# Strassen's seven products for the second feed-forward product of the last two batches

## The chip, the cores and the metric

The kernel runs on one NeuronCore of a Trainium2 chip. Its engines are TensorE (PE; the loads of its stationary operand are listed apart as PEld), VectorE (DVE), ScalarE (ACT), GpSimd (POOL) and SyncE (SP), which issues most of the DMAs. Each engine works through its own instructions in a fixed order, and semaphores hold an instruction until what it needs is there. The metric is device time in microseconds (us) of one execution.

## The reference

Eight batches of 576 tokens and 512 features go through three stages:

```python
# attention: 8 heads of 64, window of 128 keys, ALiBi slopes
scores = where(mask, q @ k.T / 8 + slope * -|i - j|, -1e9)
x = concat_heads(softmax(scores) @ v)            # 8 x 576 x 512
# Fourier mixing and a norm
u = x + real(fft(fft(x, axis=1), axis=2))
un = (u - mean(u)) / sqrt(var(u) + 1e-6)
# feed-forward
out = u + relu(un @ w_ch1) @ w_ch2               # 512 -> 2048 -> 512
```

## The kernel before

The batches b = 0 to 7 follow one another on every engine, and the stages of neighbouring batches overlap: while PE does the feed-forward products of batch b, DVE and ACT do the softmax of batch b + 1. Everything is float32 outside; where a factor goes through PE it is split into a high and a low float16 half, and a product is three passes: high by high, high by low, low by high.

The feed-forward (`ffn`, L951 to L985) takes the tokens of a batch in parts: two parts of 256 rows, and after each odd batch a third part of 128 rows, in which the remainders of two batches stand together. For a part, the first product (L965) walks over the 16 blocks of 128 hidden features, two blocks to one bank of PSUM (a "group" below): 2 blocks x 4 chunks x 3 passes = 24 matmuls of 256 columns. ACT writes the ReLU's high half (`upper_half`, L945) and DVE the low half (`lower_half`, L948) into a slot of the tile `hbuf`. When all 16 blocks are there, the second product (L979) is run for each of the two tiles of 128 rows: 16 blocks x 3 passes = 48 matmuls, `hbuf` stationary (128 x 128) and w2 streaming through with 512 columns, into one bank. One DVE instruction scales the bank and adds the residual, and a DMA writes the tile out.

The order of all instructions is written out by hand: functions put their steps into a list `waiting`, sorted by a due time (constants such as `FORWARD`, L53, one due time for the feed-forward of each batch), and the table `ORDER` says which entry of that list is taken next (`sequence()`, and the loop at its end that ties each engine to this order). DVE, ACT and POOL are recorded through one helper, so all their instructions carry the line L247 (L254 in the changed kernel); they are told apart by tiles. Other lines that matter: L295 (preparation of w1 at the start), L496 (scores), L572 to L580 (products with v), L702 and L766 (Fourier mixing, rows and columns), and the loads L269 (w), L404 (q), L405 (k) and L428 (v), which SP issues.

Names in the rows: `fp` is a bank of PSUM of the feed-forward, `sp` of the scores, `pv` of the products with v, `pd` of the Fourier mixing; `wall` holds the split weights (and other things at the start), `uT` the transposed normed rows, `X` the rows of a batch, `P` and `pt` the scores after the softmax and transposed, `fg`, `pm`, `abcd`, `fh`, `fl`, `zh`, `zl` steps of the Fourier mixing.

Of the kernel before, what the change touches and what calls it, by code (L numbers as in the profile page):

```python
# [108 lines left out]
09y1+-uRO>{9nY+CrQMaV+O_-cmlmMQM~wGc4Mks>V(#RM*DrQ+U^S>o9Oh!BwtNcJ$>QqJuy77H7?YVXxQO`+Ivn6Awuyy>LA{l
ksDqalbtEGbIR+Ra;%{EJ9@WkYE#Jb3pLKxdJc>S3+n2X&9Y&oyOhtkVtxFTRJ&s>8<4%|l*5J^!E3V~q2RpJNEO0D=coYlJL2w@  # L110
*DuPpl&bGSj=xl9VJm&RWJYV7{nYo|g-4H37T8bjtd!Y2^8|)RXpk4c^PXP7Gxv6~)wh{Hz-Nz&ef?a@ovdY}vrU&=ISILT9%W+}
^wDFs37ebT2p~p8{9aPBRP>IV_B-pH6DM=>|4Maxd_J)eh^`lmxGPoAYsIq#Pm_6+yUUf6Ae)Bg4|!ivS((K9mEeqgzm!Ek%V#We
j?XppUVdV6ljE4PIuE|T>PFA`?Knp|%@y*Q7q1kBoQn+f1Y#a_%@XgF<(VjQTIUK{P=+ZoM}0lP(kqfmx}%WSdy$8Ape0ZF@Ip4k
bx|Wvcd2?yk@b;h&(g^T&lb5AbU!m?LsRB_N*Q#{n99ap&lL<A-ZAaaBy&&5drvXY=q4r#s?@tJpJqI`7kRA^RW~Oo5(Wxt%`$r(
S6*mzZYSmwJW*#UQsytJRu+VT;-ltx+!7COq`G@ZJtHf(FR8ZT8KtwJ^D~Vjp6Qw2?6ELO@bjR1Y4M$G%e{?Fr(Qfe{;cz9y|k(O
$IscLX!5DQg-&8!Zal0~=QKU%>ABC7qTI^l<HFN}Gv*w7#<x@M5o_XE&qy{9#ur*TT)C~q??bjXL$2GDk|wu(zS1jas#M=e`P5g%
34WrjROQ?4ORGK9Je79VdM9ytn{%{Dj$I0BReqbSDK|N4a#~i*vUfSd?cP#<V}S~u?wHbc`1#SE_9uDiJNgZUs=MK)+6id(H|NiS
Vw;w}{?!|(Ro57ErlfuD>HnSVZmF{(sLov|+cVk&&lk3e-&d@7)XJ|c=-(YxGfO$x6uqP@Uyz?OW1h38t~j#SPuF;y9+W3=EgW;~
=Fz5mg{88}Ub%=mkv%B>nW*Bq5r(`HJW|Bgk>?h9k4xfcrYcWEJ(a5TPP>J2VPocM$Fy3fT!op6e#xtuDznpwuiG3i`<d}UvHv8G
NPho@az0XX?`KNLN<ueL^tV*(H)kBu>x6eYVKvhU)InA9rQ(%^p3Jg;=chPt`^K6#ahBJ!)A=*Mi~Joaqfl_IB6|~o8LL*OqsFpm  # L120
gQAE&SAEKC@jdS_*0)nWqt1RxI`P#ACqW)$L97SKU8$OEkt4&Ap0)WTN6G_Cvd#`Sr@6{(eXeIeg6c6vJ}+0^_{n9i8CAKeA3lot
;zx6Zk8<zvqxRSD%iNOGH;PlstPhHtw@bylX@)fN3R$GindQt|$}CJYlV>Nd@oUJ@M4RWX<e$|yIVsnV9u0fNF=n_sRZ5cmxK@i=
Wxt{##`Z^We6{jrrd+(KM-?}5f2uu|H+8_`BYNM`<!`zEn1(<0DQ^1z-r4`}q51y-%a6_SKf)L;y8
"""


def begin_of(p):
    b, j = divmod(p, 4)
    return BEGIN[b] + 6 * PACE[b] * j


def transform_of(b):
    return BEGIN[b] + PACE[b] * DFT
# [1053 lines left out]
```

## Time and profile before

| | us |
|---|---|
| three runs | 1024.91, 1021.87, 1024.29 (median 1024.29) |
| the profiled execution, its own time | 1021.92 |
| its span in the profile | 1020.1 |
| PE busy | 994.9 (98% of the span) |
| DVE busy | 717.0 (70%) |
| ACT busy | 565.6 (55%) |
| POOL busy | 28.5 (3%) |

The span is 1.8 us shorter than the execution's own time. The busy times are averages over the whole span; the stages differ: DVE is nearly full in some stretches and nearly idle from 870 us on, where only the feed-forward of batch 7 is left. Matmuls overlap each other in the records, so the mean duration of one matmul in the table of groups (379 ns for 512 columns) is longer than the distance from one to the next; that distance is read from the chain of waits, where a run of matmuls stands with its total time and count.

### The profile page before, as it was taken

Reading aid. Unit: us, or ns where it says so; the run is one execution under the profiler, and the core shown is the slowest. Engines: PE = TensorE matmul, PEld = TensorE weight load, DVE = VectorE, ACT = ScalarE, POOL = GpSimd, SP = SyncE. Lnnn points to the kernel's source line nnn. Section 1 sums busy time; section 2 is a strip of 40 time slices with the busy share of each in tenths; the row PEclk is TensorE's granted clock in tenths of the full one; section 3 lists DMA queues with packets and bytes.
Section 4 is the critical chain, followed back from the end, with each engine's and each line's share of the span. In section 5 each row is a group of like instructions: output and inputs, shape, how many; then the busy total and the mean of one; then the engine's idle time right before and its main releaser. Section 6 shows DMA issues by size and latency. Waiting matters only on the chain.

```text
span 1020.1 us, 23193 instructions
## 1 busy us (share of the span) xinstructions
PE 994.9 (98%) x9192; PEld 712.0 (70%) x9192; DVE 717.0 (70%) x2166; ACT 565.6 (55%) x1229; POOL 28.5 (3%) x68
## 2 busy tenths in 40 slices
PE   6998999999999999999999999999999999999998
PEld 5887767767666775858585785858586785857756
DVE  4799999896878978677988458688797793501111
...
PEclk9999999999999999999999999999999999999999
...
GB/s 357 273 255 175 40 141 83 73 156 97 135 55 139 96 133 63 93 112 57 120 95 111 53 72 97 56 91 142 126 49 101 77 45 11 63 22 1 21 11 22
DMA packets 189389, 99.86 MB, mean 98 GB/s; under 512 B 163552, under 2 KB 171744, under 8 KB 189280
## 3 DMA queue, kind: packets, MB, share of 16 engines
...
## 4 chain that ended last, share of the span: by engine, by line
PE 78%; DVE 11%; DMA 5%; ACT 3%; issue 2%; POOL 0%; SPq 0%; ACTq 0%; DVEq 0%; POOLq 0%
PE fp L965 31%; PE fp L979 31%; PE sp L496 3%; PE pd L702 3%; DVE wall L247 2%; DVE P L247 2%; PE sp L494 2%; PE pv L578 1%; DMA pt<-P 1%; PE pv L572 1%; DMA uT<-un 1%; PE pv L580 1%; PE pv L579 1%; PE pd L766 1%; ACT wall L247 1%
## 5 line engine op out<-in xcount | busy, mean ns | idle before, releaser
L979 PE MATMUL fp<-wall,hbuf 128*128 128x512 f16 x1728 | 391.8, 379 | 0.3 <-DVE hbuf L247 0.3
L965 PEld LDWEIGHTS <-wall 128*128 128x128 f16 x3840 | 339.0, 98 | 46.9 <-issue 8.1
L965 PE MATMUL fp<-uT,wall 128*128 128x256 f16 x3072 | 350.5, 273 | 3.1 <-DMA uT<-un 1.0
L979 PEld LDWEIGHTS <-hbuf 128*128 128x128 f16 x1728 | 162.4, 98 | 180.7 <-issue 2.3
L247 ACT ACTIVATE hbuf<-fp 128x512 f16<-128x512 f32 (+1 forms) x145 | 85.6, 590 | 209.5 <-PE fp L965 206.2
L247 ACT ACTIVATE P<-P,nb 128x256 f32<-128x256 f32 (+1 forms) x320 | 143.3, 478 | 74.6 <-DVE nb L247 70.8
L247 DVE SCALAR_TENSOR_TENSOR hbuf<-fp,hbuf 128x512 f16<-128x512 f32 x144 | 98.8, 686 | 95.4 <-ACT hbuf L247 94.9
L247 DVE CUSTOM_DVE_ANT_0 P<-sp,rg,nsl 128x256 f32<-128x256 f32 (+1 forms) x260 | 110.6, 450 | 13.2 <-PE sp L496 10.1
L247 DVE SCALAR_TENSOR_TENSOR P<-P 128x384 f16<-128x384 f32 (+1 forms) x104 | 63.9, 618 | 19.4 <-ACT P L247 19.3
L247 ACT ACTIVATE P<-P 128x384 f16<-128x384 f32 (+1 forms) x104 | 58.5, 570 | 22.1 <-DMA pt<-P 17.8
L247 DVE SCALAR_TENSOR_TENSOR X<-fp,misc,X 128x512 f32<-128x512 f32 x32 | 23.8, 744 | 60.7 <-PE fp L979 60.7
L578 PE MATMUL pv<-vhs,pt 128*128 128x65 f16 x468 | 54.2, 195 | 1.2 <-DMA pt<-wall 0.9
L579 PE MATMUL pv<-vl,pt 128*128 128x64 f16 x468 | 54.1, 192 | 0.0
L580 PE MATMUL pv<-vhs,pt 128*128 128x65 f16 x468 | 54.0, 193 | 0.0
L578 PEld LDWEIGHTS <-pt 128*128 128x128 f16 x468 | 43.6, 97 | 11.8 <-issue 3.7
L247 ACT ACTIVATE un<-X,nmr,rstd 128x512 f16<-128x512 f32 (+1 forms) x56 | 42.3, 804 | 13.9 <-DVE nmr L247 12.4
L579 PEld LDWEIGHTS <-pt 128*128 128x128 f16 x468 | 43.4, 99 | 5.2
L496 PE MATMUL sp<-kk,qq 64*128 64x256 f16 (+1 forms) x780 | 45.4, 260 | 0.0
L965 PE MATMUL fp<-wall,wall 128*128 128x128 f16 x768 | 44.1, 219 | 0.0
L580 PEld LDWEIGHTS <-pt 128*128 128x128 f16 x468 | 43.6, 97 | 0.0
L496 PEld LDWEIGHTS <-qq 64*128 64x128 f16 x780 | 32.7, 94 | 15.4 <-issue 10.5
L702 PE MATMUL pd<-tab_sb,fh 96*128 96x289 f16 (+1 forms) x168 | 36.8, 287 | 0.0
(178 smaller groups left out, 1206.6 us busy)
## 6 DMA issues: line engine op xcount, KB each, us to landing
...
out_dram<-X SPq DMA_DIRECT2D x32, 256.0 KB, 2.1
...
pt<-P SPq DMA_TRANSPOSE x104, 3.1
```

Of the source, the lines that this page charges most:

```text
L247: add(now[0], lambda: f(*a, **kw))
L494: T.matmul(sp[e][:m, col:col + n], lhs, keys(kk, ti), start=True, stop=True)
L496: T.matmul(sp[e][:m, col:col + n], qq[h, c0:c0 + m], keys(kk[h], ti), start=(x == 0), stop=(x == len(prods) - 1))
L572: T.matmul(pv[:, ti], pt[:, col:col + 128], vrs[p][:, e, vc], start=first, stop=last)
L578: T.matmul(pv[:, ti], ph, vh[:, e, vc], start=first, stop=False)
L579: T.matmul(pv[:, ti, 0:D], ph, vl[:, e, vc], start=False, stop=False)
L580: T.matmul(pv[:, ti], pl, vh[:, e, vc], start=False, stop=last)
L702: T.matmul(zp[:, :NS], st["in", c][l][:m, g], tab1_sb[:m, (0 if g < 2 else 2) + t, c], start=(c == 2 and p == 0), stop=(c == 1 and p == 2))
L766: T.matmul(o, st[z, g][:, j0:j0 + m], tab2_sb[:, t, gc[g]:gc[g] + gw[g]], start=(p == 0), stop=(p == 2))
L965: T.matmul(fp[:, i * n:(i + 1) * n], w1_ap(e, c, f0 + i), uT[:, j, c, 0:n], start=(c == 0 and p == 0), stop=(c == 3 and p == 2))
L979: T.matmul(op, hh[f][:, a, i * 128:(i + 1) * 128], w2_ap(e, f), start=(f == 0 and p == 0), stop=(f == 15 and p == 2))
```

## The change

For the two parts of 256 rows of batches 6 and 7, the second product is computed by Strassen's method in its seven-product form. Each part's rows are two tiles of 128, the columns of w2 two halves of 256, and the hidden blocks are taken in pairs; of this 2 x 2 by 2 x 2 block product seven products of blocks (each three passes of 128 x 128 by 256 columns: 21 matmuls a group) stand where eight were (12 matmuls of 512 columns a group). They accumulate in four banks of the scores (`sp`). What is multiplied are sums and differences of blocks:

- of the activations, once for each group of each part (`row_sums`): ACT writes the ReLU to a tile r, DVE makes four sums of 128 x 128 in a tile s, ACT copies the high half of s, DVE writes the low half. There is one r and one s, tiles named `vr`.
- of w2, once for each of the eight groups, for both batches (`second_sums`, `second_differences`, `second_halves`): six DVE instructions and two ACT copies. The results stand in tiles of the attention (`rg`, `kk`, `qq`, `P`, `pt`), the work in a tile of `X`. The constant `SUMS` puts them at a due time.
- of the seven results, once for each part (`add_up`): one ACT and seven DVE instructions where two DVE instructions were, and two DMAs.

A group's seven products come two groups behind its first product (`LAG`). The third part of 128 rows is as before. The due times of batches 6 and 7 are later, and the table of the order is another one from its first lines on. The changed lines are moved in the file: L965 is L1033 (L1088 in the third part), L979 is L1102 (third part: the same), L702 is L709, and the seven products have L1024.

```diff
@@ -50,77 +50,84 @@
 DENSE = (16, 0.08)
 STRETCH = (0.5, 0.7, 1.0, 1.15, 1.25, 1.25, 1.25, 1.25)
 BEGIN = (0.0, 8.5, 26.0, 46.4, 68.0, 90.8, 114.8, 138.8)
-FORWARD = (22, 41.6, 64.7, 88.7, 112.7, 136.7, 160.7, 184.7, 208.7)
+FORWARD = (22, 41.6, 64.7, 88.7, 112.7, 136.7, 169.7, 188.7, 208.7)
 SPIN = 2
 VLEAD = 2.4
 FIRST = (5.70, 6.00, 6.80, 6.50, 6.50)
+SEVEN = 2
+LAG = 2
+SUMS = 164.0
 ORDER = r"""
-c-q}s*{&<ObtP+-R4UCnn$LW0-@e^#_h7plZrkk)b^^md;OE5o0l(%C^5NNQ?L|sAXuvj*r-+bL
...
+c-pO7$&w?<agE#)i3BpS0|iu7*V<FP47*#ync;{sQPk4nL6jM3I`Xa)Z@kG&zb=2zUj$Gl$!IhQ
...
 """
@@ -948,6 +955,119 @@
     def lower_half(ht, fp):
         V.scalar_tensor_tensor(ht[:, 1], fp, 0.0, ht[:, 0], ALU.max, ALU.subtract)
+    quads = cycle([hbuf[:, o:o + 1024].bitcast(F16).rearrange("p (s e t) -> p s e t", s=2, e=2)
+                   for o in range(0, 4096, 1024)])
+    T2, rooms = {}, {}
+
+    def second_sums(g):
+
+        if "w" not in rooms:
+            rooms["w"] = xp.tile([128, 5, DM], F32, name="X").rearrange("p a b -> p (a b)")
+        wv, tv = rooms["w"][:, 0:1024], rooms["w"][:, 1024:2048]
+        hi, lo = wf[1][:, g, 0], wf[1][:, g, 1]
+        V.tensor_tensor(wv, hi, lo, ALU.add)
+        put(now[0] + 0.1, second_differences, g, wv, tv)
+
+    def second_differences(g, wv, tv):
+        V.tensor_tensor(view(tv, 0, (256, 2), (1, 256)), view(wv, 768, (-512, 2), (1, 256)),
+                        view(wv, 256, (-256, 2), (1, 256)), ALU.subtract)
+        V.tensor_tensor(tv[:, 512:768], wv[:, 768:1024], tv[:, 256:512], ALU.subtract)
+        V.tensor_tensor(tv[:, 768:1024], wv[:, 512:768], tv[:, 512:768], ALU.subtract)
+        put(now[0] + 0.1, second_halves, g, tv)
+
+    def second_halves(g, tv):
+        T2[g] = []
+        for x in range(2):
+            t = room_of(2 * g + x).rearrange("p (s e c) -> p s e c", s=2, e=2)
+            src = tv[:, 512 * x:512 * x + 512].rearrange("p (s c) -> p s c", s=2)
+            A.activation(t[:, :, 0], src, AF.Copy)
+            V.tensor_tensor(t[:, :, 1], src, t[:, :, 0], ALU.subtract)
+            T2[g] += [t[:, 0], t[:, 1]]
+
+    def room_of(n):
+        if n < 2:
+            return att.tile([128, 1152], BF16, name="rg", bufs=2).bitcast(F16)[:, 0:1024]
+        if n < 6:
+            return att.tile([128, 2, NQ], F16, name="qk"[n < 4] * 2).rearrange("p e t -> p (e t)")[:, 0:1024]
+        if n < 10:
+            return att.tile([128, 512], F32, name="P", bufs=PB).bitcast(F16)
+        return att.tile([128, 512], F32, name="pt", bufs=6).bitcast(F16)
+
+    def row_sums(hs, fp):
+        if "r" not in rooms:
+            rooms["r"] = [att.tile([128, 650], F32, name="vr", bufs=2)[:, 0:512] for _ in range(2)]
+        r, s = rooms["r"]
+        A.activation(r, fp, AF.Relu)
+        V.tensor_tensor(s[:, 256:384], r[:, 0:128], r[:, 128:256], ALU.subtract)
+        V.tensor_tensor(s[:, 0:128], r[:, 128:256], r[:, 384:512], ALU.add)
+        V.tensor_tensor(s[:, 128:256], r[:, 384:512], s[:, 256:384], ALU.subtract)
+        V.tensor_tensor(s[:, 384:512], r[:, 256:384], s[:, 128:256], ALU.subtract)
+        A.activation(hs[:, 0], s, AF.Copy)
+        after(0.1, V.tensor_tensor, hs[:, 1], s, hs[:, 0], ALU.subtract)
+
+    def seven(uT, tiles, slot):
+        acc = []
+        place = {1: (0, 0), 6: (0, 1), 2: (1, 0), 3: (1, 1), 4: (2, 0), 5: (2, 1), 7: (3, 0)}
+        box = []
+
+        def products(g, which):
+            h, s = box[g][:, 0], box[g][:, 1]
+            w = [(w2_ap(0, 2 * g + y)[:, 256 * x:256 * x + 256], w2_ap(1, 2 * g + y)[:, 256 * x:256 * x + 256])
+                 for y, x in ((0, 0), (1, 0), (1, 1))]
+            t3, t1, t2, t4 = [(t[:, 0], t[:, 1]) for t in T2[g]]
+            pairs = {1: (h, 0, w[0]), 2: (h, 2, w[1]), 3: (s, 3, w[2]), 4: (h, 3, t4),
+                     5: (s, 0, t1), 6: (s, 1, t2), 7: (s, 2, t3)}
+            for k in which:
+                a, o, w = pairs[k]
+                bank_, side = place[k]
+                for p, (x, y) in enumerate(((0, 0), (0, 1), (1, 0))):
+                    T.matmul(acc[bank_][:, 256 * side:256 * side + 256], a[:, x, 128 * o:128 * o + 128], w[y],
+                             start=(g == 0 and p == 0 and k in (1, 3, 5, 7)), stop=(g == 7 and p == 2 and k in (2, 4, 6, 7)))
+
+        for g in range(8 + LAG):
+            if g < 8:
+                fp = ps_f.tile([128, 512], F32, name="fp")
+                for i in range(2):
+                    for c in range(4):
+                        for p, (e, j) in enumerate(((0, 0), (0, 1), (1, 0))):
+                            T.matmul(fp[:, i * 256:(i + 1) * 256], w1_ap(e, c, 2 * g + i), uT[:, j, c],
+                                     start=(c == 0 and p == 0), stop=(c == 3 and p == 2))
+                    if i == 0:
+                        yield
+                quad = next(quads)
+                put(now[0], upper_half, quad[:, 0], fp)
+                after(0.1, lower_half, quad[:, 0], fp)
+                after(0.05, row_sums, quad[:, 1], fp)
+                box.append(quad)
+                yield
+            if g == LAG:
+                acc += [ps_s.tile([128, 512], F32, name=f"sp{x % 2}") for x in range(4)]
+            if g >= LAG:
+                products(g - LAG, (1, 6, 7))
+                yield
+                products(g - LAG, (5, 3, 4, 2))
+                yield
+        after(0.1, add_up, acc, tiles, slot)
+
+    def add_up(acc, tiles, slot):
+        if "u" not in rooms:
+            rooms["u"] = (att.tile([128, NK], F32, name="kr", bufs=1)[:, 0:512],
+                          att.tile([128, NQ], F32, name="qr", bufs=1)[:, 0:256])
+        t, u3 = rooms["u"]
+        u1, u2 = t[:, 0:256], t[:, 256:512]
+        y0, y1 = tiles
+        A.activation(u1, acc[0][:, 0:256], AF.Copy, scale=wone)
+        V.scalar_tensor_tensor(u2, acc[0][:, 256:512], wone, u1, ALU.mult, ALU.add)
+        V.scalar_tensor_tensor(u3, acc[3][:, 0:256], wone, u2, ALU.mult, ALU.add)
+        V.tensor_tensor(y0, y0, t, ALU.add)
+        V.scalar_tensor_tensor(y0, acc[1], wone, y0, ALU.mult, ALU.add)
+        V.scalar_tensor_tensor(y0[:, 256:512], acc[2][:, 256:512], wone, y0[:, 256:512], ALU.mult, ALU.add)
+        V.tensor_tensor(y1.rearrange("p (s c) -> p s c", s=2), y1.rearrange("p (s c) -> p s c", s=2),
+                        u3.unsqueeze(1).broadcast_to([128, 2, 256]), ALU.add)
+        V.scalar_tensor_tensor(y1, acc[2], wone, y1, ALU.mult, ALU.add)
+        after(0.2, nc.sync.dma_start, out=ov[slot], in_=y0)
+        after(0.25, nc.sync.dma_start, out=ov[slot + 1], in_=y1)
+
     def ffn(b):
         X = x_of(b)
         parts = [(i, 256, [X[:, XS[2 * i]], X[:, XS[2 * i + 1]]], 4 * b + 2 * i) for i in range(2)]
@@ -955,6 +1075,9 @@
             parts.append((2, 128, [uts[b // 2]], 4 * B + b // 2))
         for which, n, tiles, slot in parts:
             uT = uTs[b][which]
+            if b >= B - SEVEN and which < 2:
+                yield from seven(uT, tiles, slot)
+                continue
             per = 512 // n
             hh = []
             for f0 in range(0, 16, per):
@@ -1055,6 +1178,8 @@
     put(8.45, nc.sync.dma_start, out=exact2, in_=tab3[:, 6 * NS:])
     weights(0, 0, 0.42, 7.6, 0.2)
     weights(1, 9.5, 0.35, 16, 0.12)
+    for g in range(8):
+        put(SUMS + 0.5 * g, second_sums, g)
     traced, seen, last = nc.cur_bb.bb.instructions, 0, {}
     for i in sequence():
         seen = len(traced)
```

How the order moves, at two places. First PE, in the second product of batch 6, part 0, where it meets the row transforms of the Fourier mixing of batch 7 (`tab1_sb` is the table of the transform, `fh0` or `fh2` and `fl0` or `fl2` the halves of what is transformed, `wall0` and `wall1` the split w1 and w2). Before, and then after:

```order
L979 LDWEIGHTS hbuf_104
L979 MATMUL fp_12997<-wall1_106,hbuf_104 128x512
L702 LDWEIGHTS fh0_12941
L702 MATMUL pd_12841<-tab1_sb_92,fh0_12941 128x289
L702 LDWEIGHTS fl0_12958
L702 MATMUL pd_12841<-tab1_sb_92,fl0_12958 128x289
L702 LDWEIGHTS fh0_12941
```

```order
L1024 LDWEIGHTS hbuf_104
L1024 MATMUL sp1_12878<-wall1_106,hbuf_104 128x256
L709 LDWEIGHTS fh2_12945
L709 MATMUL pd_12976<-tab1_sb_92,fh2_12945 128x289
L709 LDWEIGHTS fl2_12971
L709 MATMUL pd_12976<-tab1_sb_92,fl2_12971 128x289
L709 LDWEIGHTS fh2_12945
L709 MATMUL pd_12976<-tab1_sb_92,fh2_12945 128x289
L1033 LDWEIGHTS wall0_105
L1033 MATMUL fp_12980<-uT_11963,wall0_105 128x256
```

Before, the streaming matmuls of 512 columns go into one bank `fp` and the first product of the part is finished; now matmuls of 256 columns go into banks `sp`, and first products (L1033) of a later group follow in between.

Second DVE, in the same stretch of the program (batch 6, part 0; `fp` feeds the ReLU, `vr` are the tiles r and s of the row sums, `X_12412` the work tile of the sums of w2). Before, and then after:

```order
L247 SCALAR_TENSOR_TENSOR hbuf_104<-fp_12787,hbuf_104 128x512
L247 TENSOR_TENSOR fg_12838<-X_11703 128x512
L247 TENSOR_TENSOR fg_12872<-X_11703 128x512
L247 SCALAR_TENSOR_TENSOR hbuf_104<-fp_12824,hbuf_104 128x512
L247 TENSOR_TENSOR fg_12872<-X_11703 128x512
L247 MEMSET pm_12888 128x4
L247 TENSOR_TENSOR pm_12888<-fg_12872 128x2x256 x2
L247 SCALAR_TENSOR_TENSOR hbuf_104<-fp_12858,hbuf_104 128x512
L247 TENSOR_TENSOR pm_12920<-fg_12838 128x2x256
L247 TENSOR_TENSOR abcd_12889<-pm_12888 128x2x128 x2
```

```order
L254 TENSOR_TENSOR X_12412<-wall1_106 128x1024
L254 TENSOR_TENSOR pt_13109<-X_12412,pt_13109 128x2x256
L254 TENSOR_TENSOR hbuf_104<-vr_12784,hbuf_104 128x512
L254 TENSOR_TENSOR pt_13108<-X_12412,pt_13108 128x2x256
L254 SCALAR_TENSOR_TENSOR hbuf_104<-fp_13047,hbuf_104 128x512
L254 TENSOR_TENSOR vr_12784<-vr_12783 128x128 x2
L254 TENSOR_TENSOR X_12412<-X_12412 128x512
L254 TENSOR_TENSOR vr_12784<-vr_12783,vr_12784 128x128
```

Before, the low halves of the ReLU stand between the steps of the Fourier mixing of the last batch; now they stand between row sums and sums of w2, and the mixing's steps come earlier and later. On SP, the first load of v (L435) is issued ahead of the first loads of q and k (L411, L412), where before it was behind them.

## Rows read from the trace of the kernel before

**Rows 1.** The page: busy times of the engines, and the granted clock in 40 slices.

```profile
PE 994.9 (98%) x9192; PEld 712.0 (70%) x9192; DVE 717.0 (70%) x2166; ACT 565.6 (55%) x1229; POOL 28.5 (3%) x68
...
PEclk9999999999999999999999999999999999999999
```

**Rows 2.** Stretches: length, busy time and count by engine, PEclk, DMA share, GB/s.

```profile
0.00:25.50 25.50, 17.28 (x100) 13.69 (x100) 11.91 (x49) 13.75 (x29) 2.07 (x13) 1.00 0.96 357
25.50:127.50 102.00, 94.96 (x763) 81.89 (x764) 92.95 (x282) 81.39 (x178) 7.47 (x9) 0.98 0.58 186
127.50:869.75 742.25, 736.17 (x7227) 516.51 (x7226) 580.40 (x1787) 447.41 (x988) 17.77 (x44) 1.00 0.44 92
869.75:1016.50 146.75, 146.45 (x1105) 99.87 (x1103) 31.03 (x51) 23.07 (x37) 1.24 (x2) 1.00 0.10 23
51.00:178.50 127.50, 121.40 (x1064) 94.47 (x1063) 122.31 (x357) 98.32 (x205) 8.09 (x11) 0.99 0.51 139
816.00:841.50 25.50, 25.50 (x255) 21.05 (x254) 23.52 (x63) 9.18 (x15) 1.31 (x3) 1.00 0.20 45
```

**Rows 3.** What PE waited for: us in total, times, longest us.

```profile
PE fp L295 <- DVE wall L247: 8.4, 2, 7.8
...
PE fp L979 <- DVE hbuf L247: 0.3, 1, 0.3
```

**Rows 4.** Chain that ended last, 900 us to the end: start us, us, what.

```profile
912.03 20.96 PE fp L965 x192
932.99 20.72 PE fp L979 x96
...
1006.11 10.38 PE fp L979 x48
...
1016.51 0.75 DVE ut L247
```

**Rows 5.** Groups by form: names, shapes, count | busy us, mean ns | idle before.

```profile
L247 DVE SCALAR_TENSOR_TENSOR hbuf<-fp,hbuf 128x512 f16<-128x512 f32 x144 | 98.8, 686 | 95.4 <-ACT hbuf L247 94.9
...
L247 ACT ACTIVATE hbuf<-fp 128x512 f16<-128x512 f32 x144 | 85.2, 592 | 209.5 <-PE fp L965 206.2 <-PE pd L222 2.7
...
L247 ACT ACTIVATE P<-P 128x512 f16<-128x512 f32 x52 | 32.2, 624 | 18.1 <-DMA pt<-P 15.6 <-DVE P L247 2.0 <-DVE r L247 0.2
L247 DVE TENSOR_TENSOR X<-pv,ri 128x320 f32<-128x320 f32 x64 | 31.1, 487 | 0.9
...
L247 DVE TENSOR_TENSOR fg<-X 128x512 f32<-128x512 f32 x32 | 21.2, 681 | 0.0
...
L247 DVE SCALAR_TENSOR_TENSOR wall<-wall,misc 128x1024 f16<-128x1024 f32 x16 | 20.4, 1277 | 0.0
...
L247 DVE TENSOR_TENSOR abcd<-pm 128x256 f32<-128x256 f32 x28 | 11.0, 416 | 0.0
```

**Rows 6.** DVE in order of time, 828 to 838 us: start us, us, instruction.

```profile
828.88 0.68 DVE L247 TENSOR_TENSOR fg<-X 128x512 f32<-128x512 f32 x1
829.48 0.68 DVE L247 SCALAR_TENSOR_TENSOR hbuf<-fp,hbuf 128x512 f16<-128x512 f32 x1
...
836.03 0.75 DVE L247 TENSOR_TENSOR abcd<-pm 128x256 f32<-128x256 f32 x2
836.71 0.68 DVE L247 TENSOR_TENSOR pm<-fg 128x512 f32<-128x512 f32 x1
```

**Rows 7.** DMA issues: line, engine, count, KB each, median us to landing.

```profile
out_dram<-X SPq DMA_DIRECT2D x32, 256.0 KB, 2.1
...
wall<-v_dram SPq DMA_DIRECT2D x4, 325.0 KB, 7.7
```

**Rows 8.** All engines in order of time, from the start.

```profile
2.11 0.60 SPq L428 DMA_DIRECT2D wall<-v_dram  x1
...
6.27 0.80 ACT L247 ACTIVATE qq<-wall,slope_sb 128x608 f32<-128x608 f32 x1 [0.56 <-DMA wall<-q_dram]
```

More of the change, by code (lines that the diff above doesn't have):

```diff
@@ L120 @@
[L120 to L123, printed above, removed]
+c-pO7$&w?<agE#)i3BpS0|iu7*V<FP47*#ync;{sQPk4nL6jM3I`Xa)Z@kG&zb=2zUj$Gl$!IhQVOTOUG8PYCp1TL~kcANPP=|??
+5LzpBSccL{#Zs_Ttf}q0<*(A7E9@GjV7rF3|B>1kY+qZuCJg+wW;=}3g+JMtjrEm>DMzl@cg5f6r?E1#`FLHYyO`aazcQ9-=&f&D
@@ new lines @@
+clHZ4b@&>ttemuxUD$IznT@`+(%Lh*6^w%x4d?w`_<8tVBiG>%Hu9Wzy72G(?D?LDg*`pBUb-+^+1WQ*cHw8?ll8v|zYhodUfaAE
+Z1KU$#@cVJbQ}|9WhJ*ZnA7j9<&HBCwvrW}UR$qM;b^lvSXo-_f7)lS6>iw0zc8D*wV7K99C2&C;r`q3O?a{2=x5~0@!T<7+j`bE
+(h%-78eRuJvoxy38niy}X;3rRom05AtE16#&pGeIZ$#6YPwcGR*!yVjYb&_MYj6E*c^_>L*3TQ(-`EK8Uf?Lcu0l`kZC5eM&PH3<
+NU=Ysl|O@B`+<~OSg)h4U?3GY_UWs*w~~cB_OZ2Z&>k=B*j@P63SOXJX1^EKLqVzr?jc??D_eUC_kyVG^bR&F)V|S*K&Pb@?8jhF
+-B|G*1WkKV547H?f3#Y&1!jtImMVB1NqaoG;yuh~MH=|L2JP#DJGbG=eP?~{nAzOg_?-pIoHb5yP~wKG0Ux|*FERR!?ev2cU*VcF
@@ new lines @@
+`E__Up7Qk{*b{nvVa*?`pq~YMm?zrf*HU`LDKl#3m{TW-2#NE9<Q=>ReStn*2RW|~+7HO$Qc~G*9gy%@T5F(2gS;##>nrxy@;6$}
+?G4$-I&mkL+=JV1Sy$T{G48E#4>S*`aN_fzBHHFQ4ybvgo`bFc$6m8dZnN_J1+Px*J+s!XGo5!!>a>H+0c&VU3CtJTX`i_Kk2XH&
+b8Rzqt?|rz4fPiK+j1{!yF!~I>4$dUNN{mwd)DcxyYNV=VrN@hSIJpm{b&v8dSlnOqzl$tk}tjYnyVVbdDzKka@X8iL9z$aHe-^O
+oZ4+^zk1gBF8N&X+x6YS?z<M>TRY5V&#S+(vI+5pE8N>qG7IjHOQMg5xz9xBnw0EJjx&|cXpqr@INfTlCZk@iOncPaxzAQ=T8lb-
+v4S1=1?hJ~9+_xATaNLQm0udYT~ijOfxhRHkxwzpUy28F_K>qLND<oo$eA7O{hbx;^iSl*R<mET#~-br2K4-aH3P5RhP9-__eK?H
@@ new lines @@
+FkBb58kd7lR<NpyywF;IbG^UtUL_vc*)^Vq)<NB8@&alqa(qD!1_ej<3t4?{692+ky1b(`?p@jUNSz3t_{<j2aiB9+`-wc0iSlKt
+|6pz1Qopx?n)fzyw~sk{S#VtN-@#gAEZhMt=hUTm29mR-Tw|1}^ygd7CF+MLdCy!OX7AQ?X;Lu|6GYCvw>R44vP5Ww-#xkcAT8oj
+ypTkk*rQv@oTKH`Dw*`SYqnZEopBv*<#M5unr%zUQ_%C!VF%3{R6q^JiLIbtTI#h{J$K@}n*8iMUs)eDpIH*uRYWvX`-J2+)-P7x
+i2GdPp}i~3C-SzB>e?<y#s{LfM%1V{PEEUANEehzGBDG<v_`Z)=;t59M=R+4H-_E5CJhIU_{!D)+6s2zBWW7KKZU=uQiQ*^l3C4H
+?QRkNIsAi_z|YR!nP`dESD{oq6*TL;&F*ilWZ_p_cb%|B2!BHq8?>WX-CtXA`L4M-ti&a~rv}682P<)fkXon0k1UbCGup6@oN;2!
@@ new lines @@
+Pt*_x;xp*81NY_!Vw*j=YC>(XCC0+*OL{h1XvYy(`i9lOYb!oGvTw&#C!^$E80?nZcSSk{qO(0mbjrPz&4=}PW3~6z%e}SvmU~tR
+w}HMd#J_v?aYzUfw0mNYPVXy?l(Y3NQTsc}$%(oW2nX6NBlQj@pO57J7kk5YO<5+SU}x6hmevzbOo?tL)>B7*`#_1sn6PfH#cN{r
+nO!w@e<HtUXT8_*7#hmNyR=I^sW7#g3Ar}v>3i!J@_%H_+V0*78v`9bP%DB8F6+@7YNanBKW`*QneMwRt*I~EmkHv^Ts(~Z$yDd}
+(9V&uYv`%<-M!K+_=K)5tY@tDTDmT3SxD_dTIXOA4GZ&Z1<&~&ZlnYABpX=qwRSTkS&v>r)KAza%wV7F;z1|?vqM|=BGI#ZX^zI$
+LcJmN9%UG`_5Ili&&5@&lQ-vcb<7a&MoeAF%AYt|BO3b3D*8Ji$;gQ^zob_L?02#i7eeMaab_zWJL9h%J>gCApw`mEOYZWDbC325
@@ new lines @@
+^^vNz>`*2xQ|R4Li&pZa@#Km-4BlJnvyhiQCED^bw>LOqq&<tX8HmMk<(7M?wM=C-MxtWZ{Z;a?-PSm*8jfA4^cpR2N23)B^6*#k
+s4{8ukTlgGtTy4?qkWxTSg%Z|5%qIY%l)xJ=)(KO({pmRqtKGGadaOe7w+#2v{F%4g7kIA*g-BEHRniyw40?}@;Sk?@Lkwww{y|e
+aX_WL+EJ>#zZ)9~beT}kbawS%-_TJ#Z7rw(ANh_PnbC^*bxuqBz_yX@xO1<F#YEDDXB^i<Cw8*28FiD}EO@?8((6voxDS;*SxEL=
+H@($rK?kRHFU<U&_pz!o#>Le)!UTc4R|xO8q-LhEBcGgcN1@$m$brr;=xNHGh<lMqJ_g2&t~ly%!@pYHC-G8~ILAFj$0>mnk60vE
+tSOhRK5MTvX&NQ1kmLuVnwm4XPTI=(JQu$eL^l&jMkCqmOjpc=^IbX@#H=S;=Ph-@z!+7b@%Ng&(>^Cci}5u_SQ%}>jMgk7SJx5f
@@ new lines @@
+wYos3xnd7JBV-d<mw__akoRB{Yp#FfY-iFA9iJ-MZp!xVFFIY_QymiL^peRytn3lHUVFadE{ybX*P{D|vYB(g2hnQBUY62bIY(Yx
+l$HFLD1ABol3G!%ifua1v7%<!BzbOSYnIZiV?v~(_6o6*HFw8t0=#KFu_CW87$*oq^ObPmS{kEDQA@X$jppT)S&Adi9>#`ij0k_E
+pBgn>l*alZvWZ!A!rBx1e;xyknrK6*EEH`$DB=d1H>B9a>RdZdgmm_dtGOKu(#wH3sUzmQp=`ryfulf=jH~xp?kHTJlQ(DLOCND3
+j8uzC6Kc$jP|jZSC{kn?T(xFo$u*(tk1fYsi-V(O&n`4oDOp-;?19|tzRM(i_oBf}7TD#hx$ss%)m4gO*WzyXtR}Kr;GYFiK%F9g
+U9zYh<1`~V*FBai;y#bEUNIW6AaX}EZNcc?p8I}O<no$4x8?VmYg`Ep97XZKz6)uTQ<8%laRRhUk<jy%t?(pjmGTT-DjuY>vGyq?
@@ L124 @@
+_@7?U&eiIzd3Co;)~tMW67TgIs^ry9UY!yQ{|74lc^dqGQ2Kvsarw&9GtsMjO}{_?`@i=V!hZo(A~Wg
 """
```

95 lines of the change are left out of this document (35 added, 60 removed).

## The prediction

> **What bounds the kernel now.** [...] Then the stretches, to see where the 25 us without PE are [rows 2]: 8.2 in the first 25.5 us, 7.0 up to 127.5, 6.1 in the next 742, 0.3 from 869.75 to PE's end; the rest, 3.6, lies behind that end. PE's waits say that the largest piece is the wait at the start for the prepared w1 (8.4 us) and that the second product waits for a low half of the ReLU for only 0.3 us in all [rows 3]. So PE's work sets the time: a matmul less is time less, as long as DVE, which has to feed the new products, keeps up. That is not a given. DVE is full in places: 122.31 of 127.5 us (96%) between 51 and 178.5, and 23.52 of 25.5 (92%) from 816 to 841.5, close ahead of the place where the new work comes in; from 869.75 on it works only 31.03 of 146.75 us [rows 2].
>
> **PE's products.** The chain of waits gives the distance between matmuls: 20.72 us for 96 of 512 columns, 215.8 ns each; 20.96 us for 192 of 256 columns, 109.2 ns each [rows 4]. The 192 have a new stationary operand before each matmul, as the seven products do, so their rate is the one to take. A group had 12 x 215.8 = 2590 ns and gets 21 x 109.2 = 2293 ns: 297 ns less. With 8 groups, 2 parts and 2 batches that is 32 x 0.297 = 9.5 us less. (An eighth of the replaced 82.9 us is 10.4; the other 0.9 is the 2.6 ns by which two matmuls of 256 columns take longer than one of 512.) The last part, of 128 rows, stays as it is, with its 48 matmuls and the 0.75 us of its residual behind them [rows 4].
>
> [...]
>
> **DVE's and ACT's new work.** Durations are those of the nearest forms [rows 5]; what counts on a full DVE is the distance from one start to the next, which is shorter: 0.60 us for 512 columns recorded with 0.68 (828.88 to 829.48), 0.34 for 256 (two in 836.03 to 836.71) [rows 6]. The line through both gives 0.205 for 128 columns and 1.13 for 1024, which no row shows in this form; bounds for 128 are 0.08 (by columns alone) and 0.28 (the recorded durations 416 and 681 ns [rows 5] carried down). Row sums: 4 x 0.205 + 0.60 = 1.42 us, 32 times, 45. Sums of w2: 1.13 + 0.60 + 2 x 0.34 + 2 x 0.60 = 3.6, 8 times, 29. Adding up: 3 x 0.34 + 4 x 0.60 less the two old instructions, 2.2, 4 times, 9. DVE goes from 717 to 800 us; ACT gets 32 x (0.592 + 0.624) + 16 x 0.624 and 2 for the adding up [rows 5], 51 us, and stays at 617. Neither reaches the span, so this costs nothing where PE's own work hides it. Where it doesn't is one stretch.
>
> **The stretch that DVE sets.** In the changed order DVE cannot run ahead of PE at its scaling of the last products with v (`ri<-pv`), shortly ahead of the piece of DVE's order shown. From there to what group 7 of batch 6, part 0, needs, DVE has 89 instructions: 32 of 128 columns, 36 of 512, 12 of 256, 3 of 1024, one of 320 and five small ones. By distances: 6.6 + 21.6 + 4.1 + 3.4 + 0.4 + 0.5 = 36.6 us; at the 96% that DVE reaches when it is the bound [rows 2], 38.1. PE has there 6 old matmuls of 512 columns, 168 of the first product, 147 of the seven products and 3 row transforms of 289: 1.3 + 315 x 0.1092 + 0.4 = 36.1 us. So PE waits 2.0 us. The bounds: 0 below (PE cannot be quicker than its own work), and above it the recorded durations [rows 5] back to back: 32 x 0.28 + 36 x 0.685 + 12 x 0.416 + 3 x 1.277 + 0.49 + 0.75 = 43.6, at 96% 45.4, a wait of 9.3. I take 2.0, since rows 6 show the distance itself. After it DVE has slack: the next 35 instructions, to the release of the four banks that part 1 needs, take 13.4 us against PE's 14.1, and `add_up` of a part (about 5 us with its waits) lies beside first products (24 matmuls, 2.6 us a group, three groups ahead of the next seven). The first sum of w2 waits for an output DMA of the tile that it reuses, 2.1 us to landing [rows 7]; DVE has not yet fallen behind there: 0, bound 1. For batch 7 nothing of the softmax is left, and the w2 sums are kept.
>
> [...]
>
> **Order and start.** The rest of the table is new too: the attention of the last batches is drawn ahead of the later feed-forward. DVE's work up to comparable points of PE's program differs by some 3 us either way, and of PE's 13 idle us between 25.5 and 869.75 [rows 2] any share could go or grow: I take 0, bounds 6 down and 9 up. At the start the load of v is issued ahead of q: its issue takes 0.60 us [rows 8], and its 325 KB [rows 7] at the 357 GB/s of that stretch [rows 2] 0.9, so q, on which ACT's first attention step waits at 6.27 [rows 8], may be up to 1.5 us later; what holds PE there is w1 [rows 3], so 0.
>
> **Sum.** 1021.92 (the profiled execution's own time; span 1020.1 and 1.8 around it) - 9.5 + 2.0 = 1014.4. The profiled execution is 2.4 us below the median of the three runs, 1024.29; set against that median the sum is 1016.8, and I say 1017. Within 0.3%, 3 us, of the median, so 1021.2 to 1027.4, counts as no change: about what a measurement of this kernel can tell.
>
> **The rivals.**
> A, the forecast: a wait of 0 to 4 us: 1014.8 to 1019 (at the median's level). For it: [rows 4, 6].
> B, DVE's distances in the new instructions are the full durations: a wait of 7.5 to 9.3 us, 1022.3 to 1024.1, or 1020 to 1022 at the level of the profiled execution. For it: the many waits of DVE on DVE; against it: in the stretch of rows 6 such chains run at 0.60.
> C, the new order also takes out some of the 13 idle us: 1009 to 1014. For it: there is something to take [rows 2]; against: DVE is the bound there and has no less to do.
> D, slower: r and s exist once, so DVE's low half waits for ACT's copy of s (0.62 us [rows 5]) and its next sums for ACT's next r. If the order fails to cover the two handovers, each of the 8 groups of the stretch costs about 2 x 0.7 us on top of its 38.1 us: 49.3, a wait of 13.2, 1028. It decides from a stretch of 48.7 us, 0.55 us for each of the 89 instead of 0.41. Against it: between the last sum and the low half 1 to 3 instructions of other work stand in most groups (the piece of DVE's order shown: 1024 and 512 columns, 1.7 us).
> E, the gain is lost to new waits outside this stretch, in the first three quarters or at the start: 1022 to 1026. For it: every instruction has moved; against: PE's waits there are small and spread.
>
> **The numbers.** A 0.62, B 0.15, C 0.10, E 0.07, D 0.06. Faster by over 0.3%: A, C and half of B, 0.80. Within: E and half of B, 0.14. Slower: 0.06. The range runs from 1009, C's lower end, to 1026, E's upper; D and what C holds below are left out.
>
> **What the changed profile would show.** Seven products at 109 ns each and PE's busy time down by about 9.5 us; the clock at the top as before. A wait of PE for `hbuf` from DVE in the second product of batch 6, part 0, of about 2 us, and none in batch 7. DVE near 96% in that stretch, at 0.2 us from one 128-column sum to the next. Up to 800 us the milestones of PE within 3 us of before. Wrong I am if the products run above 116 ns (half of the 9.5 us is gone at 32 x 21 x 7 ns), if PE waits over 6 us for DVE there, or if the idle time before 800 us changes by more than 5 us.

## The result

| | before | after |
|---|---|---|
| median of the runs compared, us | 1022.81 (1021.87 to 1024.91) | 1012.66 (1011.71 to 1013.83) |
| ratio | 1 | 0.9898, 95% interval 0.9881 to 0.9914 |
| the profiled execution, us | 1021.92 | 1013.83 |
| its span, us | 1020.1 | 1012.1 |

The change made the kernel 1.0% faster, 10.15 us between the medians. 1017 was forecast, with 1009 to 1026; the direction was right and the gain larger than the 7.3 us forecast. The profiled executions differ by only 8.1 us, since the one of after happens to be its slowest; what belongs to the change is therefore read from stretches of the trace below.

The busy times and the granted clock on the page of after, which answer to [rows 1]:

```profile
PE 985.9 (97%) x9480; PEld 742.2 (73%) x9480; DVE 801.3 (79%) x2394; ACT 609.8 (60%) x1313; POOL 32.8 (3%) x68
...
PEclk9999999999999999999999999999999999999999
```

PE lost 9.0 us of work, DVE gained 84.3 (to 801.3, 800 forecast), ACT 44.2 (51 forecast). The granted clock stands at 9 in all slices, which is 90% or more, as before.

The chain that ended last (start us, us, what), for [rows 4]:

```profile
923.78 2.62 PE fp L1033 x24
926.40 2.29 PE sp L1024 x21
...
980.44 6.88 PE sp L1024 x63
...
998.03 10.37 PE fp L1102 x48
...
1008.43 0.75 DVE ut L254
```

A group of seven products takes 2.29 us for 21 matmuls, 109.0 ns each, the rate of the first product's 2.62 us for 24. The last part is what it was: 10.37 us for its 48 matmuls and 0.75 for the residual.

The stretches of [rows 2] (length, busy time and count of PE, PEld, DVE, ACT, POOL, then PEclk, DMA share, GB/s):

```profile
0.00:25.50 25.50, 17.62 (x107) 14.80 (x108) 13.22 (x53) 15.03 (x31) 2.08 (x13) 1.00 0.96 361
25.50:127.50 102.00, 94.18 (x750) 82.23 (x749) 91.44 (x278) 80.84 (x176) 11.01 (x9) 0.97 0.60 189
127.50:869.75 742.25, 735.47 (x7282) 524.98 (x7280) 613.25 (x1860) 458.99 (x998) 17.13 (x41) 1.00 0.42 91
...
816.00:841.50 25.50, 25.07 (x250) 20.50 (x249) 25.32 (x62) 11.93 (x22) 0.52 (x1) 1.00 0.10 25
```

Up to 869.75 us PE's idle time is 7.9, 7.8 and 6.8 us, where it was 8.2, 7.0 and 6.1: the other order moved small waits about and changed their sum by 1.1. From 816 to 841.5 DVE is busy for 25.32 of 25.5 us; before it was 23.52.

What PE waited for (us in total, times, longest us), for [rows 3]:

```profile
PE fp L302 <- DVE wall L254: 8.5, 2, 6.5
...
PE fp L1102 <- DVE hbuf L254: 0.4, 1, 0.4
PE pd L709 <- DVE fl L254: 0.4, 2, 0.2
...
PE fp L1033 <- DVE hbuf L254: 0.2, 1, 0.2
```

The start still waits for w1. No row names a wait of the seven products (L1024). The two waits of 0.2 us for `fl` are those of the row transforms of the Fourier mixing in between, and the 0.2 us of L1033 for `hbuf` stand at a first product of batch 6, part 0.

The new groups on DVE (names, shapes, count | busy us, mean ns | idle before), and DVE in order of time (start us, us, instruction) through the stretch on which the forecast set its wait:

```profile
L254 DVE TENSOR_TENSOR vr<-vr 128x128 f32<-128x128 f32 x128 | 33.0, 284 | 21.1 <-ACT vr L254 20.5
...
L254 DVE TENSOR_TENSOR hbuf<-vr,hbuf 128x512 f16<-128x512 f32 x32 | 22.0, 687 | 11.4 <-ACT hbuf L254 11.4
```

```profile
822.79 0.22 DVE L254 TENSOR_SCALAR ri<-pv,psc 128x5 f32<-128x5 f32 x1
...
842.10 1.22 DVE L254 TENSOR_TENSOR X<-wall 128x1024 f32<-128x1024 f16 x1
843.23 0.28 DVE L254 TENSOR_TENSOR vr<-vr 128x128 f32<-128x128 f32 x1
843.43 0.68 DVE L254 TENSOR_TENSOR pt<-X,pt 128x512 f16<-128x512 f32 x1
844.04 0.28 DVE L254 TENSOR_TENSOR vr<-vr 128x128 f32<-128x128 f32 x1
844.24 0.68 DVE L254 TENSOR_TENSOR X<-X 128x512 f32<-128x512 f32 x1
844.84 0.68 DVE L254 SCALAR_TENSOR_TENSOR hbuf<-fp,hbuf 128x512 f16<-128x512 f32 x1
...
858.77 0.68 DVE L254 TENSOR_TENSOR hbuf<-vr,hbuf 128x512 f16<-128x512 f32 x1
```

From 842.10 to 843.23 the sum of 1024 columns takes 1.13 us to the next start although it is recorded with 1.22; from 843.23 to 843.43 and from 844.04 to 844.24 a sum of 128 columns takes 0.20, recorded with 0.28; 512 columns take 0.60. The stretch of the forecast runs from 822.79 (`ri<-pv`) to the end of the last low half of part 0, 858.77 + 0.68 = 859.45: 36.66 us, where 36.6 were added up.

PE in the same stretch (start us, us, instruction, and in brackets the idle time before it):

```profile
822.59 1.46 PE L1102 MATMUL fp<-wall,hbuf 128*128 128x512 f16 x6
824.27 5.41 PE L1033 MATMUL fp<-uT,wall 128*128 128x256 f16 x48 [0.23 <-DVE hbuf L254]
829.52 0.49 PE L1024 MATMUL sp<-wall,hbuf 128*128 128x256 f16 x3
...
836.73 0.29 PE L709 MATMUL pd<-tab_sb,fh 96*128 96x289 f16 x1
837.22 0.30 PE L709 MATMUL pd<-tab_sb,fl 96*128 96x289 f16 x1 [0.20 <-DVE fl L254]
837.35 0.29 PE L709 MATMUL pd<-tab_sb,fh 96*128 96x289 f16 x1
...
859.09 0.82 PE L1024 MATMUL sp<-wall,hbuf 128*128 128x256 f16 x6
859.75 1.15 PE L1024 MATMUL sp<-pt,hbuf 128*128 128x256 f16 x9
...
866.49 0.30 PE L709 MATMUL pd<-tab_sb,fl 128*128 128x289 f16 x1 [0.18 <-DVE fl L254]
```

The seven products begin at 829.52. The first one of group 7 that reads a row sum starts at 859.75, 0.30 us after DVE finished it. The seven products did not wait; others did, and for longer than the brackets say, since a record runs on past the start of the next matmul: the transform with `fl` is recorded from 837.22 to 837.52, and the next one starts at 837.35. Read from start to start: six matmuls of 512 columns at 215.8 ns take 1.29 us from 822.59, so the first products at 824.27 are 0.39 us late (for `hbuf`); the transform with `fl` starts 0.49 us behind the one with `fh`, where the next takes 0.13, so 0.36 us are lost. These are 0.75 us in the stretch of the forecast. The transform at 866.49, behind that stretch, loses 0.35 us in the same way.

### The profile page after: what moved, and what is told of

It is laid out like the page before. It is cut to its first block, busy times and chain, and to the rows that moved or that the text cites. A ratio compares the mean times of both kernels' runs of the same rounds, so it can differ in the third digit from the quotient of the medians.

```text
span 1012.1 us, 24134 instructions
## 1 busy us (share of the span) xinstructions
PE 985.9 (97%) x9480; PEld 742.2 (73%) x9480; DVE 801.3 (79%) x2394; ACT 609.8 (60%) x1313; POOL 32.8 (3%) x68
## 4 chain that ended last, share of the span: by engine, by line
PE 78%; DVE 12%; DMA 5%; ACT 3%; issue 2%; POOL 0%; SPq 0%; POOLq 0%; ACTq 0%; DVEq 0%
PE fp L1102 24%; PE fp L1088 24%; PE fp L1033 6%; PE sp L1024 5%; PE sp L503 4%; PE pd L709 3%; DMA pt<-P 3%; PE sp L501 2%; DVE P L254 2%; DVE hbuf L254 2%; PE pv L579 2%; DVE X L254 2%; PE pv L585 1%; PE pd L773 1%; PE pv L587 1%
## 5 line engine op out<-in xcount | busy, mean ns | idle before, releaser
L1102 PE MATMUL fp<-wall,hbuf 128*128 128x512 f16 x1344 | 304.4, 379 | 0.5 <-DVE hbuf L254 0.4
L1088 PEld LDWEIGHTS <-wall 128*128 128x128 f16 x3072 | 263.8, 98 | 31.6 <-issue 4.1
L1088 PE MATMUL fp<-uT,wall 128*128 128x256 f16 x2304 | 266.2, 273 | 1.4 <-DVE hbuf L254 1.4
L1102 PEld LDWEIGHTS <-hbuf 128*128 128x128 f16 x1344 | 125.9, 98 | 141.5 <-issue 2.3
L1033 PE MATMUL fp<-uT,wall 128*128 128x256 f16 x768 | 88.7, 273 | 0.2 <-DVE hbuf L254 0.2
L1033 PEld LDWEIGHTS <-wall 128*128 128x128 f16 x768 | 74.9, 98 | 9.5 <-DVE hbuf L254 0.7
L1024 PEld LDWEIGHTS <-hbuf 128*128 128x128 f16 x672 | 65.5, 98 | 7.7
L585 PE MATMUL pv<-vhs,pt 128*128 128x65 f16 x468 | 53.0, 195 | 3.1 <-DVE X L254 1.9
L254 ACT ACTIVATE un<-X,nmr,rstd 128x512 f32<-128x512 f32 (+1 forms) x56 | 42.3, 803 | 22.2 <-DVE nmr L254 18.6
L587 PE MATMUL pv<-vhs,pt 128*128 128x65 f16 x468 | 52.8, 193 | 0.0
L585 PEld LDWEIGHTS <-pt 128*128 128x128 f16 x468 | 43.5, 97 | 11.6 <-issue 4.3
L254 DVE TENSOR_TENSOR vr<-vr 128x128 f32<-128x128 f32 x128 | 33.0, 284 | 21.1 <-ACT vr L254 20.5
L586 PEld LDWEIGHTS <-pt 128*128 128x128 f16 x468 | 43.4, 99 | 4.5
L1024 PE MATMUL sp<-wall,hbuf 128*128 128x256 f16 x288 | 46.0, 273 | 0.0
```

The source lines that it names most:

```text
L254: add(now[0], lambda: f(*a, **kw))
L585: T.matmul(pv[:, ti], ph, vh[:, e, vc], start=first, stop=False)
L586: T.matmul(pv[:, ti, 0:D], ph, vl[:, e, vc], start=False, stop=False)
L587: T.matmul(pv[:, ti], pl, vh[:, e, vc], start=False, stop=last)
L1024: T.matmul(acc[bank_][:, 256 * side:256 * side + 256], a[:, x, 128 * o:128 * o + 128], w[y], start=(g == 0 and p == 0 and k in (1, 3, 5, 7 ...
L1033: T.matmul(fp[:, i * 256:(i + 1) * 256], w1_ap(e, c, 2 * g + i), uT[:, j, c], start=(c == 0 and p == 0), stop=(c == 3 and p == 2))
```

## The experiments

All of them start from the changed kernel. A median carries the scatter of the first 800 us: eight executions, whose programs differ only shortly ahead of there, began the second product of batch 6 between 826.39 and 830.59 us. So beside the ratio to the kernel before, I read from each trace one stretch, from the first matmul of the second product of batch 6 to the end of the last one of batch 7; in the changed kernel 829.52 to 987.32, 157.80 us.

| kernel | median us | ratio to before, 95% | the stretch, us | against after |
|---|---|---|---|---|
| after | 1012.66 | 0.9898 (0.9881 to 0.9914) | 157.80 | |
| twelve matmuls for 21, both batches | 1022.18 | 0.9979 (0.9964 to 0.9995) | 166.58 | +8.78 |
| twelve for 21, batch 6 only | 1014.95 | 0.9918 (0.9903 to 0.9934) | 161.82 | +4.02 |
| no row sums | 1011.93 | 0.9881 (0.9861 to 0.9901) | 157.06 | -0.74 |
| low half behind the copy | 1014.28 | 0.9915 (0.9897 to 0.9933) | 160.13 | +2.33 |
| 128 columns more per low half | 1014.69 | 0.9908 (0.9892 to 0.9924) | 160.63 | +2.83 |
| low half twice | 1020.92 | 0.9978 (0.9965 to 0.9990) | 165.99 | +8.19 |
| low half three times | 1036.00 | 1.0119 (1.0105 to 1.0134) | 181.49 | +23.69 |

The same differences part by part (us against after; a part ends where the matmul behind its last second product starts):

| kernel | batch 6, part 0 | batch 6, part 1 | batch 7 |
|---|---|---|---|
| twelve matmuls for 21, both batches | +2.00 | +2.03 | +4.76 |
| twelve for 21, batch 6 only | +2.00 | +2.03 | 0.00 |
| no row sums | -0.38 | -0.35 | 0.00 |
| low half behind the copy | +1.11 | +1.23 | 0.00 |
| 128 columns more per low half | +1.83 | +1.01 | 0.00 |
| low half twice | +5.57 | +2.62 | 0.00 |
| low half three times | +11.17 | +8.00 | +4.53 |

**Twelve matmuls for 21.** The eight products are put back into the changed order. The row sums and the sums of w2 stay; the adding up at the end of a part is again the two DVE instructions of before.

```diff
 def products(g, which):
+    t = 0 if 1 in which else 1
+    for i in range(2):
+        for p, (x, y) in enumerate(((0, 0), (0, 1), (1, 0))):
+            T.matmul(acc[t], h[:, x, 128 * (2*i+t):128 * (2*i+t) + 128], w2_ap(y, 2 * g + i), ...)
+    return
 ...
 def add_up(acc, tiles, slot):
+    ...                                   # the two instructions of before, then return
```

> The changed kernel and its order, but each group's 21 matmuls of 256 columns are again 12 of 512 into two banks; the row sums and the sums of w2 are still made, and nobody reads them. Theory 1 (PE's work alone sets the time): 32 groups x 297 ns come back, 9.5 us, so 1022.2, the time of the kernel before. Rival O (part of the gain is the new order's, which lessens other waits of PE): as much less as the order gives, for 3 us of order 1019.

The first matmuls of the second product in the order of time, and the chain at the last groups:

```profile
828.94 2.75 PE L1020 MATMUL sp<-wall,hbuf 128*128 128x512 f16 x12
```

```profile
979.92 2.62 PE fp L1041 x24
982.54 2.59 PE sp L1020 x12
...
987.75 7.77 PE sp L1020 x36
```

A group takes 2.59 us for its 12 matmuls, and the stretch is 828.94 to 995.52. The kernel is back at 0.2% from the one before (0.9979, interval 0.9964 to 0.9995), with 76 us more work on DVE (793.2 us) and another order. So the products carry the gain: 8.78 us of the 9.5 in the stretch, 8.3 by the ratios (0.9898 / 0.9979). The order may carry 1 or 2 us (0.5 to 3.7 by the interval); the trace doesn't show where, since PE's idle time, 26.7 us, is not below the 25.2 of before, and this piece stays open.

**Batch 6 only.** The same edit under `if slot < 28`.

> The changed kernel and its order, but batch 6 has 12 matmuls of 512 columns a group again (its row sums and the sums of w2 are still made), and only batch 7 the seven products. Theory 1: half of the 9.5 us comes back, 16 x 297 ns = 4.75 us, 1017.4, midway between the run with 12 in both batches and the changed kernel. If DVE's full stretch in batch 6 cost a hidden wait: less than half, 1014 to 1016.

The chain of waits where batch 6 ends and batch 7 begins:

```profile
911.22 2.62 PE fp L1041 x24
913.84 2.59 PE sp L1020 x12
...
921.67 2.29 PE sp L1032 x21
923.97 2.62 PE fp L1041 x24
```

2.59 us a group in batch 6, 2.29 in batch 7. In the stretch batch 6 gives back 4.02 us and batch 7 the other 4.76, where 16 x 297 ns are 4.75. In batch 6 0.7 us of the gain is lost, 0.38 in part 0 and 0.35 in part 1: as much as the two transforms that wait for `fl` lose in the changed kernel (0.36 and 0.35). In both kernels with twelve matmuls they do not wait. The ratios alone (+2.0 us) would have misled.

**No row sums.**

```diff
 def row_sums(hs, fp):
-    A.activation(r, fp, AF.Relu)
-    ...                                   # four sums, the copy, the low half
```

> The changed kernel without the row sums: ACT's two and DVE's five instructions of each group are left out, and the products read the ReLU itself, so the output is another one. DVE has 11.4 us less in the 36.6 us of batch 6, part 0. Theory 1: PE did not wait there, so no change, 1012 to 1013. My forecast's step (a wait of 2 us that DVE sets) would make it 2 us faster, 1010.5; rival B, 7 us or more faster.

The stretch is 0.74 us shorter, 0.38 and 0.35 in the two parts of batch 6, and its trace shows no wait of PE at all from 826 us on. The wait of 0.39 us for `hbuf`, ahead of the stretch, is gone too: from the first product of batch 6 to the seven products PE takes 9.98 us instead of 10.38. So 1.1 us is all that the row sums cost PE, 0.8 of it in the stretch of the forecast: no 2 us, and no 7. The ratios say -1.7 us with an interval of some 2.7 either way, and decide nothing.

**Low half twice, and three times; 128 columns more.**

```diff
-after(0.1, V.tensor_tensor, hs[:, 1], s, hs[:, 0], ALU.subtract)
+# twice or three times; or once and again for hs[:, 1, 0:128] alone
```

> The changed kernel, but DVE writes each low half of the row sums twice: 32 more instructions of 512 columns, 8 of them in the stretch that DVE fills. Theory 1 with DVE at its start-to-start distance and no slack at all in that stretch: 8 x 0.60 to 0.70 us, 4.8 to 5.6 us slower, 1017.5 to 1018.3, and nothing for the other 24. If DVE had hidden slack there (it is full only because nothing forces it to be quicker): 0 to 2 us.

> The changed kernel, but behind each low half of the row sums DVE writes its first 128 columns once more: 32 small instructions, about 0.25 us each (0.205 by distance, a little more since it waits for the one before), 8 of them in the full stretch. If DVE has no slack there at all: 8 x 0.25 = 2 us slower, 1014.7. With a slack of 1 us: 1 us slower, 1013.7. If the 8.2 us of the run with whole low halves twice came from a threshold (a long wait that lowers the clock), less than a quarter of it: 0 to 1 us.

> The changed kernel, but DVE writes each low half of the row sums three times: 64 more instructions, 16 in the full stretch. By the run with two (8.2 us for 8 x 0.73 = 5.8 us of DVE, of which 5.6 us are waits that the trace names and 1.4 us a lower clock after the longest): another 5.8 us of waits and again some for the clock, 6 to 9 us more, 1027 to 1030, so slower than the kernel before: the point from which rival D decides. If the other parts' slack takes part of it: 1024.

DVE of the kernel with the low half twice, in order of time:

```profile
832.14 1.41 DVE L1009 TENSOR_TENSOR hbuf<-vr,hbuf 128x512 f16<-128x512 f32 x2
833.47 0.69 DVE L254 SCALAR_TENSOR_TENSOR hbuf<-fp,hbuf 128x512 f16<-128x512 f32 x1
```

The two low halves start at 832.14, and the next instruction at 833.47: 1.33 us, so the pair costs 0.73 more than the one low half (0.60) did. Eight of them make 5.8 us. The 128 columns more cost 0.33 us each by the same reading, 2.6 us in eight, not the 2 that was expected. PE in that stretch, in order of time, and then PE's and DVE's busy times in pieces of 3 us (columns as above; the last three are PEclk, DMA share, GB/s):

```profile
836.77 0.30 PE L709 MATMUL pd<-tab_sb,fh 96*128 96x289 f16 x1 [0.54 <-ACT fh L254]
838.73 0.42 PE L709 MATMUL pd<-tab_sb,fl 96*128 96x289 f16 x1 [1.66 <-DVE fl L254]
...
839.19 4.22 PE L1037 MATMUL fp<-uT,wall 128*128 128x256 f16 x24
843.25 0.49 PE L1028 MATMUL sp<-wall,hbuf 128*128 128x256 f16 x3
...
864.87 0.94 PE L1028 MATMUL sp<-pt,hbuf 128*128 128x256 f16 x7 [1.25 <-DVE hbuf L1009]
```

```profile
835.00:838.00 3.00, 1.53 (x13) 0.96 (x10) 2.96 (x9) 2.32 (x4) 0.00 (x0) 1.00 0.00 0
838.00:841.00 3.00, 2.27 (x11) 1.60 (x12) 3.00 (x10) 0.16 (x1) 0.00 (x0) 0.62 0.02 5
841.00:844.00 3.00, 3.00 (x24) 2.47 (x23) 2.96 (x6) 0.96 (x2) 0.00 (x0) 0.81 0.00 0
844.00:847.00 3.00, 3.00 (x30) 2.68 (x29) 2.87 (x8) 1.82 (x5) 0.00 (x0) 1.00 0.00 0
```

The wait does not come at the products first. It comes at the row transforms of the Fourier mixing, which stand between them on PE and need `fl`, queued on DVE behind the row sums: 0.54 and 1.66 us. And PE loses more than the wait: the granted clock, 1.00 up to then, is 0.62 and 0.81 on average over the next two pieces, and the 24 matmuls from 839.19 to 843.25 take 4.06 us instead of 2.62. Then come 1.25 us at group 7's products. All of it together makes part 0 5.57 us longer, no more than the 5.8 us that DVE was given there: DVE sets the time, and the slower matmuls do not come on top. The other 2.62 us are lost in part 1, whose eight groups have 5.8 us more on DVE too (waits of 0.60, 0.91 and 0.48 us at 871.85, 911.39 and 916.63); that the other 24 groups would cost nothing holds for batch 7 alone. With 128 columns more, part 0 is 1.83 us longer for 2.6 us of DVE, with 1.17 us of wait at one `fl`, and part 1 1.01. So the slack of part 0 is under 1 us, and the smaller load already costs time.

PE's waits from 820 us on with the low half three times (us in total, times, longest us):

```profile
PE sp L1028 <- DVE hbuf L1009: 5.2, 4, 1.8
PE pd L709 <- DVE fl L254: 3.0, 2, 2.4
PE fp L1037 <- DVE hbuf L254: 2.6, 2, 2.4
PE sp L1028 <- DVE rstd L254: 2.3, 1, 2.3
```

The stretch is 23.69 us longer, 15.5 more than with two. Part 0 loses 11.17 us for 11.6 us of DVE, again about one for one; part 1 loses 8.00; and now batch 7 loses 4.53, most of it in two waits of 1.8 us at the ends of its parts, where three groups of products follow one another with no first product between them. The granted clock stands at 0.96, 0.87, 0.99 and 0.84 in the four pieces of 10 us from 830 to 870. The kernel is slower than before by 1.2%. The 6 to 9 us more that were expected came out of the 8.2 us being put down to part 0 alone. In the chain of waits low halves that overwrite one another stand at 941.10, 941.83 and 942.55 us, each with 0.70: a start 0.02 to 0.03 behind the end of the one before.

**Low half behind the copy.**

```diff
-A.activation(hs[:, 0], s, AF.Copy)
-after(0.1, V.tensor_tensor, hs[:, 1], s, hs[:, 0], ALU.subtract)
+# both issued in one step: on DVE the low half stands where the copy was put
```

> The changed kernel, but each low half of the row sums stands on DVE directly behind ACT's copy of s in the order, so less or no other work lies between the last sum and the low half. Rival D's mechanism: DVE then waits for ACT about 0.7 us a group, in the stretch of batch 6, part 0, 8 x 0.7 = up to 5.6 us slower, 1013 to 1018. If the copy is ready anyway: no change, 1012.7.

DVE's only waits for that copy between 822 and 850 us:

```profile
836.04 0.69 DVE L1008 TENSOR_TENSOR hbuf<-vr,hbuf 128x512 f16<-128x512 f32 x1 [0.36 <-ACT hbuf L1007]
...
841.43 0.69 DVE L1008 TENSOR_TENSOR hbuf<-vr,hbuf 128x512 f16<-128x512 f32 x1 [0.36 <-ACT hbuf L1007]
```

Two of 0.36 us, where rival D had 0.7 for each of eight groups; other work still stood between in most. The stretch is 2.33 us longer, 1.11 in part 0 and 1.23 in part 1. The handover costs time where the order does not cover it, but the 0.72 us of waits are not all of the 1.11: the edit also moves the low halves ahead of other work of DVE, such as one of the two `abcd` from which `fh` and `fl` are made, and the run does not tell the two apart. In the changed kernel itself DVE waits for this copy nowhere in that stretch; its first such wait is 0.25 us at 873.14.

## Why the prediction was right, and where it was not

- **The products.** 297 ns a group: 2.59 against 2.29 us in traces with the same order. 9.5 us were forecast, 8.8 arrived in the stretch, and the missing 0.7 are the two waits for `fl` in batch 6; batch 7 gave its 4.76 in full. With a weight load before each matmul the traces show 215.8 ns at 512 columns, and 109.0 at 256.
- **DVE's distances.** 36.6 us were added up for the stretch and 36.66 measured, with 1.13 and 0.20 us for the two forms that no row had shown. Rival B, full durations, is out. The waits of DVE on DVE that spoke for it don't slow it: 38 of the 90 instructions of that stretch carry one, and they start 0.08 us ahead of the recorded end of the instruction in front of them like the others. What pays, in the kernel with the low half twice, is a low half directly behind the one that it overwrites: 0.73 us more, where one low half had taken 0.60.
- **The step that failed: dividing by 96%.** The 2.0 us of wait came from 122.31 of 127.5 us in [rows 2], a stretch in which DVE was not the bound all the time: of its 5.2 idle us there the trace of before puts 4.1 down to waits for PE, ACT and POOL. Where DVE is the bound in after, it is full: busy for 25.50 of 25.5 us from 841.5 to 867, and the timeline names no idle time of DVE between 816 and 873. The step's 38.1 us should have stayed 36.6 against PE's 36.1, a wait of 0.5; from start to start PE loses 0.75 us there, and the kernel without row sums says 0.8. The places were others, too: a first product that waits for `hbuf`, and a transform that waits for `fl`, not the seven products.
- **The level.** I set the sum 2.4 us above the profiled execution, from a median of three. With five runs the median is 0.9 above it. Without both, 1021.92 - 9.5 + 0.5 + 0.9 gives 1013.8; 1012.66 was measured. The median lies below the forecast's own 1014.8 to 1019, in the piece of the range that rival C brought in: the range held by its width.
- **Order and start.** 0 was taken; PE's idle time up to 869.75 is 22.5 against 21.3 us, and the order with eight products is 0.2% from before. Rival C's idle time did not go, though the 1 or 2 us that the ratios leave to the order are not explained, and rival E's waits did not come. That the milestones up to 800 us would stay within 3 us was not so: PE's 501st matmul of the second product starts 3.4 us earlier than before, the 1001st 4.4 us later. The wait for w1 at the start is 8.5 us against 8.4: the earlier load of v cost nothing that can be seen.
- **Rival D.** Its order did not come, and its price was right for the stretch it looked at: a longer stretch of DVE costs its excess there, 11.17 us for 11.6. It left out the other parts. 48.7 us was the point where the kernel would be 3 us slower; with the low half three times the stretch is about 48.3, but part 1 and batch 7 lose another 12.5 us, and the kernel is 1.2% slower. With the low half twice (about 42.5) 8.2 of the 8.8 us that the products gave are gone, 5.6 of them in that stretch. The margin of this change is about 0.7 us of DVE for each of the 32 groups, if it is added to all of them.
